# The first unit's score maxima from unstacked key halves in row tiles, with their loads moved among the last projections

## The chip, the cores and the metric

The kernel runs on one core of one Trainium2 chip. A core has five engines with instruction streams of their own: TensorE (PE, with its weight loads shown as PEld), VectorE (DVE), ScalarE (ACT), GpSimd (POOL) and SyncE (SP), which here issues nearly all DMAs. The metric is the device time of one launch in microseconds, the median of several runs.

## The reference

Two independent blocks, joined along the last axis of the output (2048 x 896, float32):

```python
# A: a long convolution by FFT, kernel K from 256 complex modes per channel
K = 2.0 * jnp.einsum("dn,dnl->dl", C, P).real
y = jnp.fft.irfft(jnp.fft.rfft(u_t, 2 * L) * jnp.fft.rfft(K, 2 * L)[None], 2 * L)[:, :, :L]
a = y.transpose(0, 2, 1) + u * D_skip
# B: full attention, 16 heads of 28, sequence 2048, float32
qkv = (x @ wqkv).reshape(B, S, 3, H, Dh).transpose(2, 0, 3, 1, 4)
scores = jnp.einsum("bhqd,bhkd->bhqk", q, k) * Dh ** -0.5
b = (softmax(scores) @ v, heads joined) @ wo
```

The change touches block B alone: the row maxima of the scores of one of its units, which the softmax subtracts.

## The kernel before, in words

The 16 heads form four groups g of four heads j, and the 2048 queries four chunks c of 512. A *unit* is one group and one chunk: u = 4 g + c, 16 units. For each unit the kernel first finds the maximum of every query's 2048 scores, writes its negative into spare rows of the query tile (so that the score matmul already subtracts it), and then walks through the keys in 16 steps: scores, exponential on ScalarE, product with the values.

The work up to the first exponential stands in one block with three strands.

*Projections* (`transposes`, `qk_proj`, `v_proj`). For each chunk c the input is transposed, split into a part `xh` that TensorE's fast float32 format holds exactly and a rest `xl`, and multiplied with weights that are split the same way (`wh`, `wl`). A `qk_proj` is 12 matmuls into one PSUM bank of 512 columns, followed by `evac`: ScalarE writes the high part, VectorE the low part of the result into `hl`, and SP stores `hl` to DRAM (`k_d` for keys, `q_d` for queries). There are two `hl` buffers and three PSUM banks for this (`w_tile`). The order in the last chunk is four value projections, then for each group its keys and its queries. For chunks 0 and 1 of the keys, `evac` also forms the difference of the two halves of the chunk (`kb`, `dhl`) and stores it to `kd_d`.

*Seeds* (`seeds`). Eight rounds prepare the modes of block A on VectorE, ScalarE and GpSimd (tiles `tri`, `sg`, `qhat`, `px`); each ends with two stores, `sd<-sg` and `sd<-qhat`.

*Maxima of unit 0* (`max_mm`). When the projections are through, SP and ScalarE load the keys of group 0 back as four tiles `khat` of 128 rows, in which high and low parts are stacked (`load_k`, four issues for each head; ScalarE issues those of the first two heads, SP the others), then the queries of unit 1 and the values. The queries of unit 0 and the differences of group 0 are loaded earlier (`load_q(0)`, `load_kd(0)`). One matmul over the 128 stacked rows gives a tile of 128 queries by 512 keys. Each of the 16 pairs of head j and query tile t has four such tiles: `kc` 0 is the product with the difference of two key halves, `kc` 1 with the second of these halves, `kc` 2 and 3 are plain keys. ScalarE reads `kc` 0 through a relu into `rl`; VectorE adds `rl` to `kc` 1 and takes the maximum in the same instruction (max(a, b) = b + relu(a - b)); `kc` 2 and 3 are read by VectorE with a plain maximum. Five PSUM banks are used in turn. `max_join`, `max_end` and `max_put` combine the results, turn them and store them into the query tile with two issues `qhat<-mh`.

Up to here a scheduler places the instructions: it moves them within the engines' streams by its own estimate, so program order is not the order on the engines. Behind this block the order is kept as written: three tiles of unit 1's maxima (12 matmuls), then the steps of unit 0, each with one tile of maxima of the unit that follows.

DMAs use eight completion semaphores in turn, so an issue waits until the one eight before it in that order has landed; SP takes its issues strictly in order.

## Time and profile before

| | |
|---|---|
| median of 3 runs | 1362.64 us (1361.73 to 1366.7) |
| the profiled execution's own time | 1363.72 us |
| its span, first to last instruction | 1361.9 us |
| granted TensorE clock, mean | 0.976 |
| PE, DVE, ACT, POOL busy | 91%, 73%, 71%, 62% |

The profile gives start times in us from the first instruction. A row of the chain of waits has start, length, engine, destination tile and the helper's line, which is the same for every instruction here (L75), so groups are known by their tiles: `pm` and `pt` are PSUM banks of projections and maxima, `hl` the evacuated projections, `khat` keys, `qhat` queries (and, in the seeds, a borrowed buffer), `kdif` the differences, `mx`, `rl`, `m`, `mh` the maxima, `pss` the scores, `p` the exponentials, `sg` and `tri` the seeds, `sd` their place in DRAM. In a timeline a row has start, length, engine, operation, destination and sources. SPq is SP's DMA issue; its length is the issue, not the transfer.

### The profile page before, as it was taken

The numbers are of one execution on the slowest core, as the hardware profiler recorded it, in microseconds if no ns is written. First come the engines' busy times: TensorE is split into PE (matmuls) and PEld (weight loads), VectorE is DVE, ScalarE is ACT, GpSimd is POOL, SyncE is SP. The second block draws the span as 40 slices with busy tenths as digits, with TensorE's granted clock in tenths as the row PEclk, the third lists the DMA queues.
The fourth block names the chain that finished last, engine by engine and source line by source line (L and its number), as shares of the span: only waits on it lengthen the run. The fifth ranks groups of instructions, "written<-read, shape, count | busy, mean of one in ns | idle before, by whom it ended". The sixth has DMA issues, their size and how long they took to land.

```text
span 1361.9 us, 33142 instructions
## 1 busy us (share of the span) xinstructions
PE 1243.9 (91%) x12625; PEld 709.8 (52%) x12625; DVE 991.3 (73%) x2138; ACT 966.1 (71%) x2067; POOL 839.5 (62%) x705
## 2 busy tenths in 40 slices
PE   6878885799999999999999999999998999998997
PEld 5657762455555555555555555555555545544433
DVE  5897886877777777777788888888887766857311
ACT  4876752488888888888888887878786655655553
POOL 3685681278877878878888988888895111202221
PEclk9988987899999999999999999999999999999999
DMA  6677669636675545378534233632325534636476
GB/s 197 199 261 266 225 212 271 179 74 150 147 164 118 128 135 159 111 202 198 162 94 97 56 73 86 146 79 67 79 65 140 189 116 161 206 111 203 138 192 176
DMA packets 200089, 205.36 MB, mean 151 GB/s; under 512 B 95993, under 2 KB 158521, under 8 KB 197881
## 3 DMA queue, kind: packets, MB, share of 16 engines
q1 hardware_dynamic: 199544, 201.13, 53.2%
q10 hardware_dynamic: 384, 2.10, 0.6%
q8 instruction: 100, 1.64, 0.5%
q14 instruction: 61, 0.49, 0.1%
HBM read 120.73 MB, written 82.18 MB: 149 GB/s over the span
## 4 chain that ended last, share of the span: by engine, by line
PE 61%; DVE 17%; ACT 12%; issue 3%; DMA 3%; POOL 3%; SPq 0%; ACTq 0%; DVEq 0%; POOLq 0%
PE pm L75 35%; PE po L75 13%; PE pss L75 12%; ACT p L75 6%; DVE mx L75 4%; DVE g L75 2%; DVE tri L75 2%; ACT rl L75 2%; DVE p L75 2%; POOL qhat L75 1%; DVE pr L75 1%; DVE zg L75 1%; DVE rl L75 1%; DVE sg L75 1%; ACT tri L75 1%
## 5 line engine op out<-in xcount | busy, mean ns | idle before, releaser
L75 ACT ACTIVATE p<-pss 128x512 f32<-128x512 f32 x1024 | 565.4, 609 | 138.5 <-PE pss L75 127.5
L75 PE MATMUL pss<-qhat,khat 128*128 128x512 f32 x1024 | 403.1, 400 | 3.3 <-ACT p L75 3.3
L75 DVE TENSOR_REDUCE mx<-pm 128x1 f32<-128x512 f32 x500 | 321.4, 683 | 116.3 <-PE pm L75 115.1
L75 PE MATMUL pm<-khat,qhat 128*128 128x512 f32 x749 | 330.1, 444 | 41.4 <-DVE mx L75 36.5
L75 POOL TENSOR_TENSOR e<-e,sdb 128x256 f32<-128x256 f32 x168 | 201.8, 1201 | 171.9 <-ACT e L75 162.9
L75 PE MATMUL po<-p,v 128*32 128x512 f32 x2048 | 271.9, 599 | 0.0
L75 POOL TENSOR_TENSOR e<-e,eu 128x256 f32<-128x256 f32 x168 | 248.1, 1477 | 13.2
L75 PEld LDWEIGHTS pm<-khat,qhat 128*128 128x128 f32 x749 | 142.0, 190 | 216.0 <-DVE mx L75 79.8
L75 PEld LDWEIGHTS pss<-qhat,khat 128*128 128x128 f32 x1024 | 191.1, 189 | 46.7 <-ACT p L75 11.2
L75 DVE CUSTOM_DVE_ANT_0 rl<-pm,rl 128x512 f32<-128x512 f32 x249 | 171.4, 688 | 48.3 <-ACT rl L75 43.8
L75 POOL TENSOR_TENSOR eu<-e,sdb 128x256 f32<-128x256 f32 x168 | 201.7, 1201 | 0.0
L75 DVE TENSOR_TENSOR g<-g,zg 128x128 f32<-128x128 f32 x392 | 162.9, 416 | 46.3 <-ACT zg L75 41.3
L75 ACT ACTIVATE rl<-pm 128x512 f32<-128x512 f32 x249 | 151.2, 607 | 20.7 <-PE pm L75 18.8
L75 POOL TENSOR_TENSOR p<-pr,pr 64x448 f32<-64x448 f32 x32 | 40.9, 1277 | 191.6 <-DVE pr L75 180.5
L75 PE MATMUL pm<-kdif,qhat 128*128 128x512 f32 x249 | 101.6, 408 | 2.2 <-DVE mx L75 1.5
L75 PEld LDWEIGHTS pm<-e,g 128*32 128x32 f32 x3584 | 63.0, 110 | 52.8 <-issue 30.8
L75 DVE TENSOR_TENSOR zg<-g,zg 128x128 f32<-128x128 f32 x224 | 87.5, 391 | 1.9
L75 PEld LDWEIGHTS po<-p,v 128*32 128x32 f32 x2048 | 56.6, 110 | 42.7 <-issue 38.0
L75 PE MATMUL pm<-xh,wh 112*128 112x512 f32 x128 | 56.8, 448 | 22.3 <-DVE hl L75 10.8
L75 PE MATMUL pm<-e,g 128*32 128x64 f32 x3584 | 72.5, 220 | 0.0
L75 ACT ACTIVATE y<-pm 128x448 f32<-128x448 f32 x48 | 26.3, 548 | 63.0 <-PE pm L75 30.7
L75 DVE TENSOR_TENSOR pr<-pm,ub 128x448 f32<-128x448 f32 x64 | 37.0, 619 | 32.7 <-PE pm L75 32.7
(137 smaller groups left out, 1571.8 us busy)
## 6 DMA issues: line engine op xcount, KB each, us to landing
sdb<-sd SPq DMA_DIRECT2D x56, 336.0 KB
qhat<-q SPq DMA_DIRECT2D x64, 256.0 KB
khat<-k SPq DMA_DIRECT2D x56, 256.0 KB
sd<-sg SPq DMA_DIRECT2D x8, 1456.0 KB
k<-hl SPq DMA_DIRECT2D x16, 512.0 KB
q<-hl SPq DMA_DIRECT2D x16, 512.0 KB
mw<-in_mw SPq DMA_DIRECT2D x16, 512.0 KB
sd<-qhat SPq DMA_DIRECT2D x8, 896.0 KB
```

Of the source, the lines that this page charges most:

```text
L75: i = f(*args, **kw)
```

## The change

Unit 0's maxima no longer use the stacked tiles. Five tiles `own_*` of 128 rows by 2 x 512 hold the high and the low parts of all four heads side by side: the queries of unit 0, the differences of the halves of the first two chunks (`d`), the second halves of these chunks (`b`), and the same two for the other chunks. SP loads them among the last projections, at the slots in `OWN`. They lie where the projections' `y_p` pool lay, which is closed at the first key projection of the last chunk.

Since the halves are not stacked, a score tile is the sum of four products (high and low of queries with high and low of keys), each over the 32 rows of one head (`own_max`): 256 matmuls instead of 64, issued for two heads in turn, whose rows lie in different 32-row strips of the array.

All keys are now read in pairs (`PAIRS` = 2): `kc` 0 and 2 are differences and go through ScalarE's relu, `kc` 1 and 3 are second halves and go through VectorE's add-and-maximum. For this the second difference is needed for group 0, so `evac` forms it for chunks 2 and 3 too (`kd2_d`); its temporaries `kb` and `dhl` now come from the `rl` ring.

The weights `wh`, `wl` are four tiles in the buffers that `khat` takes later, and all four `load_k(0, ...)` are issued by SP.

In the order that the scheduler gives the changed kernel, SP's stream near the end of the projections is: the store of the last chunk's first keys, `sd<-sg`, `own_q` and the first difference, the first query store, `sd<-qhat`, the first second-halves tile (two issues), the second group's key and query stores, a row block of `qhat`, the third group's key store, another row block, the second difference and the other second-halves tile (two issues), the third group's query store, `sd<-sg`, two row blocks, the fourth group's key store, `sd<-qhat`, its query store, 16 `khat`, 4 `qhat`, 4 `v`, the last `sd<-sg` and `sd<-qhat`, and then `qhat<-mh`. On TensorE six matmuls of the first own pair stand ahead of the last but one projection and the other two ahead of the last one. On ScalarE the two relu reads of this pair stand between the evacuations of the second group's queries and the third group's keys.

```diff
--- before.py
+++ after.py
@@ -42,6 +42,7 @@
 SGB, XB, XL = 2, 5, 4
 K0, KP, KD, UP = 0, 3.5, 5, 3
 A0, A1 = 26, 34
+OWN, KIND, PAIRS = (31, 31, 32, 34, 34), "dbdb", 2
 
 N1 = 32
 N2 = 64
@@ -103,6 +104,7 @@
     dram = ctx.enter_context(tc.tile_pool(name="dram", bufs=1, space=DRAM))
     k_d = [dram.tile([2, 128, L], F32, name=f"k_{g}") for g in range(G)]
     kd_d = [dram.tile([2, 128, CQ], F32, name=f"kd_{g}") for g in range(G)]
+    kd2_d = dram.tile([2, 128, CQ], F32, name="kd2")
     q_d = [[dram.tile([2, 128, CQ], F32, name=f"q_{g}_{c}") for c in range(NQ)] for g in range(G)]
     sd_d = [dram.tile([BO, 128, SDF], F32, name=f"sd_{o}") for o in range(NO)]
     yu_d = dram.tile([128, N1, D], F32, name="yu_d")
@@ -130,6 +132,7 @@
     q_p = pool(att, "q_p", side="right")
     v_p = pool(att, "v_p", side="right")
     kd_p = pool(att, "kd_p", side="right")
+    k0_p = pool(k0_st, "k0_p", side="right")
 
     def mm32(o, w, x_, start, stop, at=0):
 
@@ -140,10 +143,10 @@
 
     kt_g, kd_g, q_u, m_u, mh_u, o_u, rl_u = {}, {}, {}, {}, {}, {}, {}
 
-    def load_k(g, j, p, queue=nc.sync):
+    def load_k(g, j, p):
         t = p.tile([128, L], F32R, name="khat", bufs=HG)
         for r in range(4):
-            queue.dma_start(t[32 * r:32 * r + 32, :].bitcast(F32), k_d[g][r % 2, 32 * j:32 * j + 32, :])
+            nc.sync.dma_start(t[32 * r:32 * r + 32, :].bitcast(F32), k_d[g][r % 2, 32 * j:32 * j + 32, :])
         kt_g.setdefault(g, []).append(t)
 
     v_g = {}
@@ -169,24 +172,30 @@
 
     def max_mm(u, i, kc, ps=w_tile):
 
-        if i == 0 and kc == 0:
-            m_u[u] = q_p.tile([128, HG, 4, 3], F32, name="mx", bufs=2)
         j, t = divmod(i, 4)
         pm = ps()
         q, kt = q_u[u][:, j, t * 128:(t + 1) * 128], kt_g[u // NQ][j]
-        mx = m_u[u][:, j, t, max(kc - 1, 0):max(kc - 1, 0) + 1]
         if kc == 0:
             nc.tensor.matmul(pm, q, kd_g[u // NQ, j], start=True, stop=True)
-            rl_u[u, i] = kd_p.tile([128, CQ], F32, name="rl", bufs=2)
-            nc.scalar.activation(rl_u[u, i], pm, AF.Relu)
         elif kc == 1:
             kb = kt.rearrange("p (c s n) -> p c s n", c=NQ, s=2)[:, :2, 1, :]
             nc.tensor.matmul(pm.rearrange("p (c n) -> p c n", c=2), q, kb, start=True, stop=True)
-            rl = rl_u.pop((u, i))
-            nc.vector.tensor_tensor_reduce(rl, pm, rl, 1.0, -3.0e38, ALU.add, ALU.max, mx)
         else:
             nc.tensor.matmul(pm, q, kt[:, kc * CQ:(kc + 1) * CQ], start=True, stop=True)
-            nc.vector.tensor_reduce(mx, pm, axis=AX.X, op=ALU.max)
+        max_read(u, i, kc, pm)
+
+    def max_read(u, i, kc, pm, pairs=1):
+        if u not in m_u:
+            m_u[u] = q_p.tile([128, HG, 4, 4 - pairs], F32, name="mx", bufs=2)
+        j, t = divmod(i, 4)
+        if kc // 2 < pairs and kc % 2 == 0:
+            rl_u[u, i] = kd_p.tile([128, CQ], F32, name="rl", bufs=2)
+            nc.scalar.activation(rl_u[u, i], pm, AF.Relu)
+        elif kc // 2 < pairs:
+            rl = rl_u.pop((u, i))
+            nc.vector.tensor_tensor_reduce(rl, pm, rl, 1.0, -3.0e38, ALU.add, ALU.max, m_u[u][:, j, t, kc // 2:kc // 2 + 1])
+        else:
+            nc.vector.tensor_reduce(m_u[u][:, j, t, kc - pairs:kc - pairs + 1], pm, axis=AX.X, op=ALU.max)
 
     def max_join(u):
         m_u[u, 1] = q_p.tile([128, HG * 4], F32, name="m1", bufs=2)
@@ -212,7 +221,6 @@
         s_p = pool(sst, "s_p")
         x_p = pool(xst, "x_p")
         y_p = pool(wst, "y_p", side="right")
-        w_p = pool(wst, "w_p", side="right")
         ps_w[0] = pool(st, "ps_w", 1, PSUM)
         ps_t = pool(st, "ps_t", 2, PSUM)
         ps_n = pool(st, "ps_n", 2, PSUM)
@@ -227,12 +235,12 @@
                 nc.sync.dma_start(xns[c, h], xs[:, 2 * h:2 * h + 2, :])
 
         load_x(0)
-        wh = w_p.tile([CK, 2, NCK, H, 32], F32R, name="wh")
-        wl = w_p.tile([CK, 2, NCK, H, 32], F32R, name="wl")
+        wh, wl = ([k0_p.tile([128, L], F32R, name="khat", bufs=HG)[:CK].rearrange("p (k h e) -> p k h e", k=NCK, h=H)
+                   for _ in range(2)] for _ in range(2))
         vh = y_p.tile([CK, NCK, D], F32R, name="vh")
         vl = y_p.tile([CK, NCK, D], F32R, name="vl")
-        for w in (wh, wl):
-            nc.gpsimd.memset(w[:, :, :, :, DH:].bitcast(F32), 0.0)
+        for w in wh + wl:
+            nc.gpsimd.memset(w[:, :, :, DH:].bitcast(F32), 0.0)
         vst = [x_p.tile([128, H, 32], F32, name=f"vst{i}") for i in range(2)]
         for t in vst:
             nc.gpsimd.memset(t[:, :, DH:DH + 1], 1.0)
@@ -271,8 +279,8 @@
         for k in range(NCK):
             for s in (1, 0):
                 src = wns[k][:, s, :].rearrange("p (h e) -> p h e", e=DH)
-                nc.scalar.activation(wh[:, s, k, :, :DH], src, AF.Copy)
-                nc.vector.tensor_tensor(wl[:, s, k, :, :DH], src, wh[:, s, k, :, :DH].bitcast(F32), ALU.subtract)
+                nc.scalar.activation(wh[s][:, k, :, :DH], src, AF.Copy)
+                nc.vector.tensor_tensor(wl[s][:, k, :, :DH], src, wh[s][:, k, :, :DH].bitcast(F32), ALU.subtract)
             nc.scalar.activation(vh[:, k, :], wns[k][:, 2, :], AF.Copy)
             nc.gpsimd.tensor_tensor(vl[:, k, :], wns[k][:, 2, :], vh[:, k, :].bitcast(F32), ALU.subtract)
 
@@ -450,7 +458,7 @@
             n = 0
             for k in range(NCK):
                 for w_, x_ in ((wh, xh), (wl, xh), (wh, xl)):
-                    nc.tensor.matmul(pp, w_[:, s, k, hs, :].rearrange("p h e -> p (h e)"), x_[k],
+                    nc.tensor.matmul(pp, w_[s][:, k, hs, :].rearrange("p h e -> p (h e)"), x_[k],
                                      start=n == 0, stop=n == 3 * NCK - 1)
                     n += 1
 
@@ -463,16 +471,16 @@
                 else:
                     nc.scalar.activation(th, pp, AF.Copy)
                     nc.vector.tensor_tensor(tl, pp, th.bitcast(F32), ALU.subtract)
-                if s == 1 and c < 2:
+                if s == 1 and (c < 2 or g == 0):
                     HC = CQ // 2
-                    kb = y_p.tile([128, HC], F32, name="kb")
-                    dhl = y_p.tile([128, 2, HC], F32R, name="dhl")
+                    kb, dhl = (kd_p.tile([128, CQ], F32, name="rl", bufs=2) for _ in range(2))
+                    kb, dhl = kb[:, :HC], dhl.bitcast(F32R).rearrange("p (i l) -> p i l", i=2)
                     dh, dl = dhl[:, 0], dhl[:, 1]
                     nc.scalar.activation(kb, pp[:, HC:], AF.Copy)
                     nc.vector.tensor_tensor(kb, pp[:, :HC], kb, ALU.subtract)
                     nc.scalar.activation(dh, kb, AF.Copy)
                     nc.gpsimd.tensor_tensor(dl, kb, dh.bitcast(F32), ALU.subtract)
-                    nc.sync.dma_start(kd_d[g][:, :, c * HC:(c + 1) * HC].rearrange("i p l -> p i l"), dhl.bitcast(F32))
+                    nc.sync.dma_start((kd_d[g] if c < 2 else kd2_d)[:, :, c % 2 * HC:(c % 2 + 1) * HC].rearrange("i p l -> p i l"), dhl.bitcast(F32))
                 nc.sync.dma_start((k_d[g][:, :, c * CQ:(c + 1) * CQ] if s == 1 else q_d[g][c]).rearrange("i p l -> p i l"),
                                   hl.bitcast(F32))
             return evac
@@ -492,10 +500,43 @@
                 nc.sync.dma_start(v_d[c][:, :, t], vs.rearrange("p (g h) e -> p g (h e)", g=G))
             return evac
 
+        own, own_p = {}, []
+
+        def own_open():
+            wst.close()
+            own_p.append(pool(wst, "own_p", side="right"))
+
+        def own_load(n):
+
+            own[n] = t = own_p[0].tile([128, 2, CQ], F32R, name=f"own_{n}")
+            f = lambda d: d.rearrange("i p l -> p i l")
+            if n == "q":
+                nc.sync.dma_start(t.bitcast(F32), f(q_d[0][0]))
+            elif KIND[n] == "d":
+                nc.sync.dma_start(t.bitcast(F32), f(kd_d[0] if n == 0 else kd2_d))
+            elif KIND[n] == "b":
+                for c in range(2):
+                    c0 = (n - 1 + c) * CQ + CQ // 2
+                    nc.sync.dma_start(t[:, :, c * CQ // 2:(c + 1) * CQ // 2].bitcast(F32), f(k_d[0][:, :, c0:c0 + CQ // 2]))
+            else:
+                nc.sync.dma_start(t.bitcast(F32), f(k_d[0][:, :, n * CQ:(n + 1) * CQ]))
+
+        def own_max(t, js, kc, ps):
+            pms = [p() for p in ps]
+            for n, (a_, b_) in enumerate(((0, 0), (0, 1), (1, 0), (1, 1))):
+                for j, pm in zip(js, pms):
+                    r = slice(32 * j, 32 * j + 32)
+                    nc.tensor.matmul(pm, own["q"][r, a_, t * 128:(t + 1) * 128], own[kc][r, b_, :],
+                                     start=n == 0, stop=n == 3, tile_position=(32 * j, 0))
+            for j, pm in zip(js, pms):
+                max_read(0, 4 * j + t, kc, pm, PAIRS)
+
         work = []
         for c in range(NQ):
             jobs = [lambda c=c, s=s, g=g: qk_proj(c, s, g) for g in range(G) for s in (1, 0)]
             v_jobs = [lambda c=c, t=t: v_proj(c, t) for t in range(4)]
+            if c == NQ - 1:
+                jobs[0] = (lambda f: lambda: (own_open(), f())[1])(jobs[0])
             jobs = v_jobs + jobs if c == NQ - 1 else jobs + v_jobs
             jobs[0] = (lambda c, f: lambda: (transposes(c), f())[1])(c, jobs[0])
             if c + 1 < NQ:
@@ -516,6 +557,9 @@
         for i in range(2):
             ahead[A1 + i].append(lambda i=i: load_q(0, range(2 * i, 2 * i + 2)))
 
+        for t, n in zip(OWN, ("q", 0, 1, 2, 3)):
+            ahead[t].append(lambda n=n: own_load(n))
+
         def project():
 
             e = work.pop(0)() if work else None
@@ -531,18 +575,20 @@
                 f()
             if t + 1 == PW:
                 project()
-                wst.close()
-                k0_p = pool(k0_st, "k0_p", side="right")
                 for j in range(HG):
-                    load_k(0, j, k0_p, nc.scalar if j < 2 else nc.sync)
+                    load_k(0, j, k0_p)
                 load_q(1)
                 for c in range(NQ):
                     load_v(0, c)
         xst.close()
         more = [lambda: ps_t.tile([128, CQ], F32, name="pt")] * 2 + [w_tile] * 3
-        for i in range(16):
-            for kc in range(4):
-                max_mm(0, i, kc, more[(4 * i + kc) % 5])
+        n_ = 0
+        for t in range(4):
+            for js in ((0, 1), (2, 3)):
+                for kc in range(4):
+                    own_max(t, js, kc, [more[(n_ + i) % 5] for i in range(2)])
+                    n_ += 2
+        wst.close()
         max_join(0)
         max_end(0, ps_t.tile([128, CQ], F32, name="pt"))
         max_put(0)
```

## The prediction

> **What bounds the kernel now.** I read the page's span, then the chain of waits between the last projections and the first exponential, then a table by stage, then the DMA queue of SP and the window of the DMA engines. The whole run is 1361.9 us of span; the execution itself took 1363.72 us, 1.1 us above the median of 1362.64 that is shown. The change touches only the stage up to about 260 us; behind it the instruction order is unchanged, so what counts is when the first exponential starts.
>
> ```profile
> span 1361.9 us, 33142 instructions
> ```
>
> The chain of waits (start, length, what it was):
>
> ```profile
> 196.12 7.99 PE pm L75 x24
> 204.11 6.44 DMA khat<-k
> ...
> 210.93 6.78 DMA qhat<-q
> ...
> 225.82 0.60 DVE rl L75
> 226.42 1.21 DVE mx L75 x3
> ...
> 250.79 0.21 DVE m L75
> ...
> 258.59 0.60 ACT rl L75
> ```
>
> ```profile
> 260.50 1.09 ACT L75 ACTIVATE p<-pss 128x512 f32<-128x512 f32 x2
> ```
>
> The last two projections end at 204.1 us. Then TensorE stands until 217.9, because keys and queries of the first unit are still in the DMA. The 64 maxima of the unit follow up to 250.8, paced by VectorE: three reads per tile, 0.60 us each (1.81 us for one rl and two mx). The join, twelve matmuls of unit 1 and the table load fill 250.8 to 260.5, where the first exponential starts (the last row is from the timeline). Now the stages, in columns PE, PEld, DVE, ACT, POOL busy, then the granted clock, DMA share, GB/s:
>
> ```profile
> 193.00:196.00 3.00, 0.00 (x0) 0.00 (x0) 2.05 (x4) 3.00 (x6) 0.98 (x1) 0.74 0.16 61
> 196.10:204.10 8.00, 7.98 (x24) 6.25 (x24) 6.74 (x16) 3.01 (x10) 6.53 (x12) 0.68 0.84 266
> 204.10:217.90 13.80, 0.26 (x2) 0.08 (x1) 3.39 (x6) 2.23 (x6) 3.67 (x4) 0.65 1.04 286
> 217.90:250.80 32.90, 26.01 (x64) 12.76 (x64) 29.28 (x65) 9.55 (x16) 0.00 (x0) 0.89 0.97 270
> ```
>
> The reader should see two things. VectorE has no slack from 217.9 to 250.8 (29.28 of 32.90 us). And the DMA engines are full from 204 to nearly 250. The next fence says what stands in that queue (SP's issues, start and length) and when it runs dry (window 240 to 256 in 40 slices of 0.4 us: the 9s end in the twentieth slice, at about 248.2).
>
> ```profile
> 199.42 0.38 SPq L75 DMA_DIRECT2D k<-hl  x1
> ...
> 210.57 0.80 SPq L75 DMA_DIRECT2D qhat<-q  x2
> ...
> 215.45 11.04 SPq L75 DMA_DIRECT2D khat<-k  x8
> 226.97 3.82 SPq L75 DMA_DIRECT2D qhat<-q  x4
> 231.75 3.83 SPq L75 DMA_DIRECT2D v<-v  x4
> ...
> 237.74 0.37 SPq L75 DMA_DIRECT2D sd<-qhat  x1
> 251.67 1.26 SPq L75 DMA_DIRECT2D qhat<-mh  x2
> ```
>
> ```profile
> DMA  9999999999999999999941000000000010077799
> ```
>
> The maxima go back into the query rows by qhat<-mh, and no score of the unit can start before these land. Before, they are issued at 251.67 into an empty queue.
>
> **The change part by part.** *Reads.* Both key halves in pairs: per tile two reads on ScalarE (0.60 us, the rl row at 258.59) and two on VectorE (0.60) instead of one and three. 16 tiles make 19.3 us on each engine, where VectorE had 33 us (217.9 to 250.8). Alone this would be worth up to 13 us, and it is off the limit afterwards.
>
> *Matmuls.* 64 matmuls over 128 rows become 256 over 32 rows (four products of hi and lo), in pairs of heads on two row strips. No row strip runs in the trace of before, so I bound one of them by the nearest rows:
>
> ```profile
> 197.57 0.63 PE L75 MATMUL pm<-xh,wh 112*128 112x512 f32 x1
> 197.99 0.63 PE L75 MATMUL pm<-xh,wl 112*128 112x512 f32 x1
> ...
> 201.36 0.40 PE L75 MATMUL pm<-xh,wh 112*128 112x512 f32 x1
> 201.59 0.39 PE L75 MATMUL pm<-xh,wl 112*128 112x512 f32 x1
> ```
>
> ```profile
> 278.92 0.86 PE po L75 x8
> ```
>
> Start to start, a full-width matmul of 512 columns takes 0.23 us at full clock and 0.42 at half. Eight on four column strips take 0.86 us, 0.108 each, so strips do overlap. Lower end 0.117 (two strips fully overlapped), upper end 0.23 (no overlap). I take 0.125, as the strip row lies near the lower end: 31 us, and 3 us for the first 24, which the built order does not interleave by strips. The Trainium skill, "TensorE: Matmul & The Clock Gate", section Part 3 on row and column tiling, gives 3.07 times for four row tiles at 512 columns; by 77% efficiency it would be 0.15 us each, 39 us, an estimate that no run here shows yet.
>
> *Where they start.* The loads that the maxima need no longer follow the last projection: the queries, both differences and both key halves come as five tiles of 512 KB on SP (seven issues: the two key tiles take two each), queued between the seed stores, the hl stores and the rows of the first unit's queries. In the built order the last pieces (second difference, second half) stand right behind the store that was issued at 199.42 (k<-hl of the third head group). So the 13.8 us hole goes, if SP gets to that store as early as now.
>
> *It does not.* The built order puts two things ahead of it. First, VectorE now takes the low part of the query projection before it (second group) after three sg operations that stood behind it before:
>
> ```profile
> 195.38 0.69 DVE L75 TENSOR_TENSOR hl<-pm,hl 128x512 fp32r<-128x512 f32 x1 [0.57 <-ACT hl L75]
> ...
> 198.65 0.74 DVE L75 SCALAR_TENSOR_TENSOR hl<-pm,kones,hl 128x512 fp32r<-128x512 f32 x1
> ```
>
> It moves from 195.4 to after 198.65, plus 0.4 for the added difference (below): until about 199.7, where its bank comes free and the last but one projection can start (196.12 before). Second, ScalarE stands at two relu reads of the first pair before it may evacuate that third group, and TensorE finishes this pair only behind the last but one projection. So: 199.7 plus 12 matmuls at 0.42 (TensorE has been idle, clock 0.74 and 0.68 in the rows 193 to 204) is 204.8; two more pair matmuls, 205.6; two reads of 0.60, 206.9; evacuation by ScalarE and VectorE, 0.60 and 0.74, 208.3. The store that SP issued at 199.42 leaves at about 208.3, 8.9 us later, and everything behind it on SP with it. The last projection waits for the same bank and ends at 208.3 + 5.1 = 213.4 instead of 204.1. If TensorE is at full clock, 2.3 us of this goes (12 x 0.19); if the reads cost nothing, 1.2 us more.
>
> *The added differences* (two more groups):
>
> ```profile
> L75 ACT ACTIVATE kb<-pm x8: 363/374/387, 23.5 to 100.9; 128x256 f32<-128x256 f32 x8
> L75 DVE TENSOR_TENSOR kb<-pm,kb x8: 404/417/426, 24.4 to 102.3; 128x256 f32<-128x256 f32 x8
> L75 ACT ACTIVATE dhl<-kb x8: 401/416/425, 24.8 to 102.8; 128x256 fp32r<-128x256 f32 x8
> L75 POOL TENSOR_TENSOR dhl<-kb,dhl x8: 740/1168/1932, 25.3 to 106.9; 128x256 fp32r<-128x256 f32 x8
> ```
>
> Twice 0.79 us on ScalarE, 0.42 on VectorE, 1.2 on POOL and a store of 256 KB. The one near 180 us lies where VectorE sets the chain, so 0.4 us (in the sum above); the earlier one hides in the DMA waits of 193 to 196. At most 2 x 2.4 us if none is hidden.
>
> *DMA.* What drains when: rates come from two windows, 32-partition loads (226 to 232) and stores and 128-partition loads (240 to 242):
>
> ```profile
> DMA packets 244, 1.34 MB, mean 223 GB/s; under 512 B 81, under 2 KB 81, under 8 KB 81
> ```
>
> ```profile
> DMA packets 430, 0.78 MB, mean 391 GB/s; under 512 B 46, under 2 KB 96, under 8 KB 429
> ```
>
> The sizes in KB per issue (q<-hl is as k<-hl, and a v load of 128 rows by 512 floats is 256 KB):
>
> ```profile
> qhat<-q SPq DMA_DIRECT2D x64, 256.0 KB
> khat<-k SPq DMA_DIRECT2D x56, 256.0 KB
> sd<-sg SPq DMA_DIRECT2D x8, 1456.0 KB
> k<-hl SPq DMA_DIRECT2D x16, 512.0 KB
> ...
> sd<-qhat SPq DMA_DIRECT2D x8, 896.0 KB
> ```
>
> From the store at 199.42 to the first qhat<-mh stand: 16 khat and 7 qhat issues (1.18 us each), four hl stores (1.34), four v loads (0.67), two seed stores sd<-sg (3.8) and two sd<-qhat (2.35). That is 27.1 + 5.4 + 2.7 + 7.6 + 4.7 = 47.5 us, from 199.4 to 246.9; the queue ran dry at 248.2, so the sum holds within 1.3 us. The change adds two of its five loads behind that store (2.7 us); the other three go into the hole from 193 on (share 0.16). From 208.3: 208.3 + 47.5 + 2.7 + 1.0 = 259.5 us, when the last seed store has gone. The built order has qhat<-mh behind it on the same queue. All khat loads are on SP now, ahead of it too, while eight were issued by ScalarE.
>
> *The sum.* TensorE ends its maxima at 213.4 + 31 + 3 - 1 (the eight done before) = 246.4, and qhat<-mh is ready to issue about 1 us later (250.8 to 251.67 before). It lands only behind the queue: 259.5 + 1.5 = 261.0 (0 to 3 us for the landing; I take the middle), and then one score and the exponential, 0.8 us: 261.8 instead of 260.5. The twelve matmuls of unit 1 and the table load, which stood in the path before, lie in the shadow of this wait; if it goes, they are late next, and the start is the end of the maxima plus 9.7 us (250.8 to 260.5), 256.1. So the gain of 14 us at the start and 13 us of reads is given back, first to later projections, then to a full DMA queue. 1363.72 + 1.3 = 1365.0 in the profiled execution's terms, 1364 in terms of the median.
>
> **The rivals.** *A, slower: the row strips do not overlap.* The start is set by TensorE once the maxima end after 252.1, that is from 0.155 us per matmul, not far above the value taken. At 0.23, 248 matmuls end at 213.4 + 57.0 = 270.4, the first exponential starts at 280.1, 1383 us. For it: no row strip in the trace, and the same 57 us if the strips overlap but the clock stays at half. Against it: the overlap of the column strips, and TensorE would have no idle time to lose its clock in. At 0.18 it is 1370.
>
> *B, faster: the projections do not slip.* If the relu reads find their pair done early and TensorE is warm, the store leaves at about 201, the queue is dry at 252 and the exponential starts at 254.5: 1356.6. For it: the six early pair matmuls may fill the idle time of 193 to 196 and keep the clock up; against it: the order of the built ScalarE queue.
>
> *C, the early maxima do not start early,* since the second difference and half land late (about 215 us by the queue above). It costs TensorE about 2 us at 213 to 217 and changes nothing as long as the DMA ends later.
>
> The Trainium skill, "TensorEngine Tiling (Array Packing)", section Key Properties, says that a change of tiling mode drains TensorE; that is a few changes here, and no row prices it.
>
> **How the numbers follow.** The forecast has 0.48, A 0.26, B 0.22, C within the forecast and the rest 0.04. A measurement of this kernel can tell about 0.5%, 6.8 us, from no change. Of B, 0.17 is over 6.8 us faster, with 0.01 of the forecast; of A 0.24 is over 6.8 us slower (the rest stays at 0.16 to 0.18 us a matmul), with 0.06 of the forecast if both unknown costs of the added groups show. That makes 0.18 faster, 0.52 same, 0.30 slower. The range goes from B's 1356 to 1377, a matmul of 0.21 us in A; about 0.1 is left out on each side. The forecast alone: 1359 to 1369.
>
> **What would show it.** Right: the last projection ends near 213; a DMA row of 9s until about 259; the first p waiting for DMA qhat<-mh; own matmuls at 0.12 to 0.13 us start to start. Wrong: k<-hl of the third group at about 201 (B); or TensorE busy with own tiles until 260 or later, at 0.2 us each or a granted clock near 0.5 (A). Were qhat<-mh to land before the last seed store is through, the queue would not be in order, and the start would be 256.

## The result and the profile after

The changed kernel takes 1379.93 us (median of four runs, 1379.77 to 1380.37), the kernel before 1363.58 beside it: a ratio of 1.0129, interval 1.0102 to 1.0155. It is slower, and outside the predicted range of 1356 to 1377. The profiled execution took 1379.77 us with a span of 1378.0. The first exponential starts at 273.18 instead of 260.50, so 12.7 of the 16.1 us are lost where the prediction looked for them; the other 3.4 come later (see the end of the experiments).

```profile
273.18 1.09 ACT L76 ACTIVATE p<-pss 128x512 f32<-128x512 f32 x2
```

The chain of waits of the changed kernel, from the last projections to the first exponential (start, length, engine, tile):

```profile
194.27 5.49 PE pm L76 x12
199.76 0.77 PE pt L76 x2
...
201.01 0.59 ACT rl L76
201.60 0.58 ACT hl L76
202.21 0.76 DVE hl L76
203.01 6.28 PE pm L76 x16
...
210.48 0.66 DVE hl L76
211.18 2.08 PE pm L76 x4
...
260.05 1.30 PE pm L76 x7
...
265.85 5.40 PE pm L76 x9
271.28 0.60 ACT rl L76
```

From 211.18 to the end of the maxima at 261.4 the chain is TensorE but for 1.5 us, where it was VectorE before. No DMA stands in it. The table by stage says why (PE, PEld, DVE, ACT, POOL busy with counts, which take in what overlaps an edge, then granted clock, DMA share, GB/s):

```profile
201.00:207.60 6.60, 4.58 (x11) 3.62 (x12) 5.22 (x13) 2.05 (x7) 2.81 (x3) 0.50 0.58 153
207.60:211.00 3.40, 1.68 (x7) 0.78 (x5) 2.75 (x7) 1.13 (x4) 3.24 (x4) 1.00 0.99 331
211.00:220.00 9.00, 7.34 (x29) 5.46 (x31) 2.68 (x8) 2.29 (x5) 0.07 (x1) 0.50 1.06 355
220.00:230.00 10.00, 10.00 (x51) 8.13 (x50) 3.99 (x14) 3.12 (x7) 0.00 (x0) 0.50 1.06 280
...
240.00:250.00 10.00, 10.00 (x60) 7.50 (x56) 4.38 (x13) 3.37 (x6) 0.00 (x0) 0.50 1.03 247
250.00:261.40 11.40, 11.40 (x59) 8.20 (x55) 4.79 (x16) 4.56 (x8) 0.00 (x0) 0.50 0.55 195
```

TensorE is busy without a pause from 220 to 261.4, and its granted clock is 0.50 all that time. It had been 1.00 for a moment (207.6 to 211.0), in which TensorE then stood for 1.91 us, waiting for the evacuation that frees a PSUM bank (timeline); it never came back.

```profile
211.18 1.22 PE L76 MATMUL pm<-own,own_q 32*128 32x512 f32 x2 [1.91 <-DVE hl L76]
```

The last 244 of the 256 own matmuls need 50 us, about 0.20 each. VectorE and ScalarE, 4.4 and 3.4 of 10 us, are far from the limit. SP's issues and the DMA window from 240 to 260 (40 slices of 0.5 us), both of the changed kernel, show that the queue isn't the limit either:

```profile
202.99 0.38 SPq L76 DMA_DIRECT2D k<-hl  x1
...
245.90 0.37 SPq L76 DMA_DIRECT2D sd<-qhat  x1
263.88 1.27 SPq L76 DMA_DIRECT2D qhat<-mh  x2
```

```profile
DMA  8979999999999999999999999999999610000000
```

The queue runs dry at about 255.5; the maxima are stored only at 263.88, into an empty queue.

### The profile page after: what moved, and what is told of

It is laid out like the page before. It is cut to its first block, busy times and chain, and to the rows that moved or that the text cites. A ratio compares the mean times of both kernels' runs of the same rounds, so it can differ in the third digit from the quotient of the medians.

```text
span 1378.0 us, 33610 instructions
## 1 busy us (share of the span) xinstructions
PE 1273.5 (92%) x12817; PEld 736.6 (53%) x12817; DVE 984.9 (71%) x2140; ACT 976.6 (71%) x2087; POOL 838.7 (61%) x709
## 4 chain that ended last, share of the span: by engine, by line
PE 64%; DVE 15%; ACT 12%; issue 3%; POOL 3%; DMA 2%; SPq 0%; ACTq 0%; DVEq 0%; POOLq 0%
PE pm L76 38%; PE po L76 13%; PE pss L76 12%; ACT p L76 6%; DVE mx L76 3%; DVE g L76 2%; ACT rl L76 2%; DVE p L76 2%; PE pt L76 2%; DVE tri L76 1%; DVE pr L76 1%; POOL qhat L76 1%; DVE qhat L76 1%; DVE sg L76 1%; DVE zg L76 1%
## 5 line engine op out<-in xcount | busy, mean ns | idle before, releaser
L76 DVE TENSOR_REDUCE mx<-pm 128x1 f32<-128x512 f32 x480 | 308.4, 683 | 108.3 <-PE pm L76 107.1
L76 PE MATMUL pm<-khat,qhat 128*128 128x512 f32 x720 | 318.5, 444 | 39.6 <-DVE mx L76 35.2
L76 PEld LDWEIGHTS pm<-khat,qhat 128*128 128x128 f32 x720 | 136.5, 190 | 211.3 <-DVE mx L76 76.1
L76 DVE CUSTOM_DVE_ANT_0 rl<-pm,rl 128x512 f32<-128x512 f32 x260 | 178.6, 689 | 64.7 <-ACT rl L76 43.5
L76 ACT ACTIVATE rl<-pm 128x512 f32<-128x512 f32 (+1 forms) x268 | 159.9, 598 | 33.1 <-PE pm L76 23.0
L76 PE MATMUL pm<-xh,khat 112*128 112x512 f32 x256 | 93.9, 451 | 23.5 <-DVE hl L76 11.4
L76 PE MATMUL pm<-kdif,qhat 128*128 128x512 f32 x240 | 96.8, 403 | 0.7 <-DVE pr L76 0.2
L76 PEld LDWEIGHTS pm<-xh,khat 112*128 112x128 f32 x256 | 54.6, 219 | 39.9 <-DVE hl L76 13.5
```

The costliest lines, as they stand in the source:

```text
L76: i = f(*args, **kw)
```

## The experiments

The question was why 256 matmuls on two row strips keep half the clock, and whether that is the whole error. The theories, as the expectations number them: 1, the clock follows the number of rows at work, and two strips of 32 are too few; 2, matmuls of 32 rows never release it; 3, strips do not overlap beyond two; 4, the stage starts cold, and a clock that is full stays full while there is no gap; 5, formed after the first eight runs, what counts is the share of rows at work over some microseconds. All runs in one table (clock and first exponential from the run's profile, the time a median, or one value for e2, e3, e4, f4 and g3; the kernel before has its first exponential at 260.5, and 1361.8 to 1363.6 us beside these runs):

| run | what it changes | clock in the own stage | first exponential | time, us |
|---|---|---|---|---|
| after | | 0.50 | 273.2 | 1379.9 |
| e1_four | four strips in turn, eight banks | 0.50 and 1.00 in turn | 270.5 | 1373.2 |
| e2_full | the same count over 128 rows | 1.00 | 277.7 | 1380.2 |
| e3_rows64 | the same count over 64 rows | 0.50 | 329.9 | 1436.3 |
| e4_warm | 48 full-row matmuls added | 1.00 | 262.8 | 1366.6 |
| f3_warm16 | 16 of them, ahead of all | 1.00, 0.50 from 219 | 273.0 | 1380.2 |
| f1_order | written order, first key pairs first | 0.50 from 208 | 265.7 | 1370.2 |
| f2_late | f1 with two seed stores later | 0.50 from 211 | 267.2 | 1374.0 |
| f4_pairs1 | f1 with one pair instead of two | 0.50 from 210 | 267.6 | 1375.5 |
| g0_banks | f1 with other banks | 0.50 from 210 | 259.3 | 1364.6 |
| g1_one | g0 with one full-row matmul a group | 1.00 from 213 | 275.2 | 1377.7 |
| g2_two | g0 with two a group | 1.00 from 214 | 283.4 | 1385.1 |
| g3_cold | after with two a group | 1.00 from 219 | 282.2 | 1382.6 |
| h0_hi | after with one product of four | 0.50 | 257.0 | 1360.9 |
| h1_fill | g0 with full rows in its two gaps, then eight banks | 1.00 to 239 | 257.1 | 1363.9 |
| h2_hi | g0 with one product of four | 0.50 | 256.1 | 1357.7 |
| h3_hi_late | h2 with two seed stores later | 0.50 | 254.8 | 1359.5 |

**How many rows.** e1_four takes four heads at a time, over eight PSUM banks instead of five:

```diff
-            for js in ((0, 1), (2, 3)):
-                for kc in range(4):
-                    own_max(t, js, kc, [more[(n_ + i) % 5] for i in range(2)])
+            for kc in range(4):
+                own_max(t, (0, 1, 2, 3), kc, [more[(n_ + i) % 8] for i in range(4)])
```

> Edit: the maxima of unit 0 are issued for all four heads in turn (four row strips of 32, eight PSUM banks in rotation) instead of two heads and five banks. Theory 1 (the clock follows how many rows of the array work at a time, and two strips are too few): the granted clock goes to about 1.0 a few us into the own matmuls, which then take 0.06 us each or wait for the reads (22 us for all); they end near 235 us, and the start of the exponentials is set by the DMA queue, about 256 us, so 1359 to 1362 us, 18 to 21 us below the changed kernel. Theory 2 (32-row matmuls never release the clock, however many strips): clock 0.5 throughout, 0.107 us each, end near 243 us; the time is much the same, since the DMA queue still ends later. Theory 3 (the strips beyond two do not overlap): 0.214 us each as in the changed kernel, end near 262 us, 1380 us.

e2_full and e3_rows64 keep count and order, and let each matmul run over all 128 rows or over the first 64. What they subtract in unit 0 is another value, so they are read for time alone.

```diff
-  matmul(pm, own["q"][r, a_, ...], own[kc][r, b_, :], ..., tile_position=(32 * j, 0))
+  matmul(pm, own["q"][:, a_, ...], own[kc][:, b_, :], ...)                            # e2
+  matmul(pm, own["q"][:64, a_, ...], own[kc][:64, b_, :], ..., tile_position=(0, 0))  # e3
```

> Edit: each of the 256 matmuls contracts over all 128 rows (the four heads summed), so the value that is subtracted in unit 0 is another one; count, banks and order are kept. Theory 1 and theory 2: the granted clock is about 1.0 in this stage, matmuls do not overlap and take 0.23 us each, 60 us in all, first exponential near 281 us, about 1387 us. Theory 4 (the clock stays at half because the stage starts cold, whatever runs in it): clock 0.5, 0.43 us each, 110 us, about 1437 us.

> Edit: each of the 256 matmuls contracts over rows 0 to 63 (two heads summed; the subtracted value is another one), one after the other, so that 64 rows work at any time, as with two overlapping strips. Theory 1: clock 0.5 as in the changed kernel, now 0.43 us each, 110 us, first exponential near 330 us, about 1437 us. If the number of working rows does not matter but their tiling in strips of 32 does: clock 1.0, 0.23 us each, about 1387 us.

The same stage in these three (columns as above), e1 first, then e2 and e3:

```profile
232.00:238.00 6.00, 5.16 (x42) 4.08 (x35) 2.62 (x8) 2.78 (x6) 0.00 (x0) 0.50 1.06 219
238.00:244.00 6.00, 4.59 (x41) 2.88 (x36) 3.83 (x11) 2.79 (x6) 0.00 (x0) 0.93 1.04 219
```

```profile
232.00:238.00 6.00, 6.00 (x28) 4.97 (x27) 1.89 (x5) 2.05 (x4) 0.00 (x0) 1.00 1.00 225
```

```profile
232.00:238.00 6.00, 6.00 (x15) 4.58 (x14) 1.31 (x4) 1.09 (x2) 0.00 (x0) 0.50 1.04 227
```

With TensorE equally full (6.00 of 6), 128 rows hold the full clock and 64 rows one at a time stay at half. The two did not enter the stage alike: the projections had raised e2's clock to 1.00 at 204.9, while e3's fell to 0.50 at 213.0. So this compares holding with not raising; but projections over 112 rows, equally full, do raise the clock (in after, 3.41 us without a pause at 0.50, then 1.00 from 207.6). Occupancy alone doesn't decide, then, and it isn't the 32-row form as such. e3 also settles the overlap: without it a matmul takes 0.42 us at half clock; two strips took half of that. Four strips start four matmuls every 0.43 us at half clock, 0.11 each (e1_four, from 229.8), so theory 3 falls; and they raise the clock at times, though they wait for reads in between (5.16 and 4.59 of 6 us), so theory 2 falls too. e1 ends 11 us above what theory 1 let expect, at 1.0073 (1.005 to 1.0096) of before.

**History.** e4_warm puts 48 full-row matmuls (three runs of 16, results unused) at the start, of which the built order places 32 ahead and 16 among the first own ones; f3_warm16 puts only 16, all ahead.

```diff
+        for i in range(3):                       # f3_warm16: range(1)
+            pd = w_tile()
+            for n in range(16):
+                nc.tensor.matmul(pd, own["q"][:, 0, :128], own[0][:, 0, :], start=n == 0, stop=n == 15)
```

> Edit: 48 matmuls over 128 rows are added, 32 ahead of the own maxima and 16 among the first of them, results unused. Theory 1: the clock rises to 1.0 during these and falls back to 0.5 within some 5 us of two-strip work; own matmuls end about 10 us later than in the changed kernel, about 1388 us. Theory 4: once at 1.0 it stays there, own matmuls take 0.107 us each, 27 us in all, end near 252 us, about 1370 us.

> Edit: 16 matmuls over 128 rows ahead of the own maxima, results unused; everything else as in the changed kernel. Theory 4 (two strips keep a full clock but can't raise a half one): the clock reaches 1.0 before or within these and stays there, 0.107 us per own matmul; the maxima end near 244 us, the DMA queue near 253 us sets the rest, first exponential 254 to 256 us, 1358 to 1361 us, at or just below the kernel before. If the 16 that stood amid the own matmuls in the run with 48 were what kept the clock: back to 0.5 after some 7 us, end of the maxima near 260 us, about 1378 us.

e4_warm by stage:

```profile
232.00:238.00 6.00, 6.00 (x56) 4.86 (x54) 4.03 (x14) 3.96 (x8) 0.00 (x0) 1.00 1.04 228
244.00:250.00 6.00, 6.00 (x53) 4.71 (x52) 4.32 (x13) 3.61 (x7) 0.00 (x0) 1.00 1.05 280
```

The same two strips, back to back, now keep 1.00 for over 25 us, at 0.117 each (205 start from 226 to 250): 48 more matmuls, and 13 us less than after. f3_warm16 starts its own matmuls warm too (stages, then one row of its timeline):

```profile
213.00:218.00 5.00, 5.00 (x32) 3.71 (x33) 2.48 (x6) 1.69 (x3) 0.00 (x0) 1.00 1.08 363
...
219.50:225.00 5.50, 5.49 (x24) 4.86 (x27) 1.31 (x4) 2.13 (x4) 0.00 (x0) 0.50 1.11 376
```

```profile
219.51 1.21 PE L76 MATMUL pm<-own,own_q 32*128 32x512 f32 x2 [0.79 <-DVE mx L76]
```

The clock is gone at 219.1, until 270, and nothing is gained (1.0125, 1.0096 to 1.0155). TensorE stands there for 0.79 us, as VectorE was late with one read, but this stand is not shown to be the cause. e4_warm kept its clock through one nearly as long:

```profile
225.00 0.73 PE L76 MATMUL pm<-own,own_q 32*128 32x512 f32 x3 [0.69 <-ACT rl L76]
```

In f3_warm16, before the stand, the strips had come one at a time, from 215.8 to 217.5 with starts 0.23 to 0.34 us apart. So theory 4 holds in its first half, and "no gap" is not the condition; the last section takes this up.

**The written order.** f1_order keeps the order of the maxima as written on all engines, and takes the first key pairs of all tiles before the second, whose loads land later. f2_late also moves the last two seed stores behind `qhat<-mh`. f4_pairs1 is f1 without the second difference, so that `kc` 2 and 3 are plain keys read by VectorE.

```diff
+        nc.kept = KEPT["a"]
+        for half in range(2):
             for t in range(4):
                 for js in ((0, 1), (2, 3)):
-                    for kc in range(4):
+                    for kc in (2 * half, 2 * half + 1):
```

```diff
+                if t >= n_stage - 2:             # f2_late
+                    seeds_late.append(f)         # called behind max_put(0)
-OWN, KIND, PAIRS = (31, 31, 32, 34, 34), "dbdb", 2
+OWN, KIND, PAIRS = (31, 31, 32, 34, 34), "dbkk", 1   # f4_pairs1
```

> Edit: the own maxima keep their written order on all engines, so none of them stands between the projections, and the pair of the first key halves is taken for all tiles before the second. Theory 4: TensorE goes from the projections into the own maxima without a gap and at full clock, 27 us, end near 232 to 236 us; the store of the third group's keys leaves near 199 to 201 us, the DMA queue runs dry near 250 to 252 us and qhat<-mh lands behind it; first exponential 252 to 255 us, 1355 to 1358 us. If the clock is lost at a gap between the last projection and the own maxima, it stays at 0.5 and the maxima end near 262 us, about 1378 us.

> Edit: as the run with the written order, and the last two seed stores (2.4 MB) are issued behind qhat<-mh instead of ahead of it. If the wait of qhat<-mh in SP's queue is what gives the gain back, it lands some 6 us earlier, near 246 us, and the first exponential starts at 248 to 252 us (the loads of unit 1's queries and its twelve matmuls then decide), 2 to 5 us below the run with the written order. If that queue isn't the limit: no difference.

> Edit: as the run with the written order, but only the first two key chunks are read in pairs (VectorE reads three of four score tiles, as before the change), and the second difference is neither formed nor loaded. VectorE's 48 reads take 29 us, TensorE's matmuls 27 us; the maxima end 2 to 4 us later than with both pairs, near 236 to 240 us, still ahead of the DMA queue: within 2 us of the run with the written order. If the reads are the limit: 5 us or more above it.

f1_order's timeline of TensorE:

```profile
205.77 1.19 PE L76 MATMUL pt<-own,own_q 32*128 32x512 f32 x8
...
209.91 2.07 PE L76 MATMUL pm<-own,own_q 32*128 32x512 f32 x7 [2.73 <-DVE hl L76]
```

The projections end at 205.8 at full clock and the own matmuls start without a pause, and then one PSUM bank is still held by an evacuation (2.73 us). From 208 on the stage runs at 0.50; the first exponential is still 7.5 us ahead of after's. The start gives little of this (16 matmuls are done at 213.6, in after 12 at 214.0); the last 240 take 41.0 us instead of 47.7 at the same clock, as the strips overlap more closely in this order. f2_late stands 4.70 us at the same place and gains nothing: with the store of the maxima ahead of 6 us of seed stores, the first exponential is not earlier (267.2 against 265.7), so the queue wasn't the limit, and in the profiled executions some 4.5 us more than in f1 are lost later. f4_pairs1, a single run, reaches the first exponential 1.9 us later than f1 and takes 5.4 us more in all; VectorE is nearly full there (13.86 of 15 us):

```profile
240.00:255.00 15.00, 15.00 (x93) 11.70 (x88) 13.86 (x23) 0.00 (x0) 0.00 (x0) 0.50 1.00 296
```

So reading the second half in pairs is worth about 2 us of this stage while TensorE sets the pace; the rest of the 5.4 us is lost behind it, and its cause was not looked for.

**Banks and fillers.** g0_banks takes two banks `pn` into the turn and only every fifth from the projections' ring. g1_one and g2_two add one or two full-row matmuls ahead of every group of eight own ones (eight ahead of groups 1 and 5); g3_cold adds two to every group of the changed kernel and nothing else.

```diff
-        more = [pt] * 2 + [w_tile] * 3
+        more = [pt] * 2 + [pn] * 2 + [w_tile]
+            for n in range(fill):       # g1 1, g2 and g3 2; not in g0
+                nc.tensor.matmul(pd, own["q"][:, 0, :128], own[0][:, 0, :], start=True, stop=True)
```

> The kernel with the written order of the maxima (f1_order), with the two banks pn as well and only one bank of the projections' in every five, so that the second and third group of eight own matmuls need not wait for the last evacuations (2.73 us before the row at 209.91 in that run). Theory 4 (a clock that is full stays full as long as the row strips run without a gap): if the new banks close the gap, the clock stays at 1.0 from 200.5 on, 32 groups of 8 x 0.107 = 27.5 us end the maxima near 237, the first exponential starts between 253 (where the DMA queue is the limit) and 256, 1356 to 1359. What I expect rather: the reads of the first tiles on ScalarE stand behind an evacuation that waits for its buffer until 210.94, so a gap of 1.5 to 3 us only moves to the third or fourth group, the clock is lost between 208 and 214 as before, and the time is 1368 to 1372.

> As g0_banks, with one matmul over all 128 rows (its result is not used) ahead of every group of eight own matmuls, and eight instead of one ahead of the first and of the fifth group, where the reads are late. Theory 5 (what counts in a window of 3.4 us is the share of rows at work: 1 for a matmul over 128 rows, a half for two strips, none in a gap; the full clock is kept and regained well above one half and not at one half): a group has 0.21 + 0.86 us with a mean share of 0.6, the gaps are filled with full rows, so the clock stays at 1.0 or comes back within two windows; 32 x 1.07 + 14 x 0.22 = 37.3 us from 205.8, maxima end at 243 to 247, first exponential at 253 to 257, 1356 to 1361: faster than both kernels. Against it (any two-strip stretch of 0.86 us at half clock 1.7 us holds the clock down, however it is mixed): half clock, 2.14 us a group, maxima end near 280, 1390 or more.

> As g1_one with two full-row matmuls ahead of every group. Theory 5: mean share of rows 0.67, clock 1.0 with more room for gaps; 32 x 1.28 + 12 x 0.22 = 43.7 us, maxima end at 250 to 252, first exponential at 259.5 to 262, 1363 to 1366. If one full-row matmul per group is too few and two are enough, this one is faster than g1_one, which then has half-clock stretches; if neither is, 2.57 us a group, 1400 or more.

> The changed kernel in its own order and with its own banks, with two full-row matmuls ahead of every group and nothing else, so the stage starts at half clock as there (0.50 from 211.0 on). Theory 5: the share of rows is 0.67 instead of 0.50 at the same full occupancy, so the clock rises to 1.0 within two or three windows of 3.4 us and stays there unless a gap of more than 1.5 us comes; maxima end near 211.2 + 6 + 27 groups x 1.28 = 252, first exponential 260 to 264, 1366 to 1372, although 64 matmuls are added. If only an unmixed stretch of full-row matmuls lifts the clock (theories 1 and 2 in their strict form): half clock to the end, 32 x 2.57 = 82 us, first exponential near 303, 1410.

g3_cold by stage:

```profile
212.00:216.00 4.00, 3.56 (x8) 2.31 (x8) 0.44 (x1) 0.99 (x3) 0.00 (x0) 0.50 1.06 393
216.00:220.00 4.00, 4.00 (x14) 2.42 (x14) 1.30 (x3) 0.00 (x0) 0.00 (x0) 0.58 1.05 320
220.00:225.00 5.00, 5.00 (x26) 2.84 (x23) 0.00 (x0) 0.15 (x1) 0.00 (x0) 1.00 1.09 341
```

The clock rises from cold to 1.00 at 219.3, and it stays there to 274. The rise itself doesn't test the mixture, since the scheduler had put three groups' full rows in one stretch just ahead of it:

```profile
216.45 2.93 PE L76 MATMUL px<-own,own_q 128*128 128x512 f32 x6
```

What the run shows is that two full-row matmuls to eight own ones keep the clock, not that they raise it; that only an unmixed stretch raises it, as the strict form of theories 1 and 2 has it, is not refuted by this run. The times are 10 to 20 us above the expected ranges in all three: at the full clock a group takes 1.56 (g1_one) to 1.66 us (g2_two), where after's eight matmuls at half clock take 1.6. g2_two's timeline shows where it goes:

```profile
230.98 0.73 PE L76 MATMUL px<-own,own_q 128*128 128x512 f32 x2
231.64 0.49 PE L76 MATMUL pn<-own,own_q 32*128 32x512 f32 x1
...
232.76 0.73 PE L76 MATMUL px<-own,own_q 128*128 128x512 f32 x2
```

From one pair of full-row matmuls to the next is 1.78 us here and 1.66 on average (29 pairs from 220 to 268). Two at 0.227 (e2_full, 176 from 220 to 260) and eight at 0.117 (e4_warm) make 1.39; the other 0.27 to 0.39 us goes at the two changes between 128 rows and strips, 0.13 to 0.2 each. In g1_one the same sum gives 0.2. The prediction had named the Trainium skill, "TensorEngine Tiling (Array Packing)", section Key Properties, for the drain at a change of mode, as something that no row priced: these 0.13 to 0.2 us, 64 times over, fit it, though what TensorE does in them is not shown. g0_banks halves the stands of f1 (its timeline):

```profile
207.25 0.50 PE L76 MATMUL pt<-own,own_q 32*128 32x512 f32 x1 [0.94 <-ACT rl L76]
...
214.65 0.79 PE L76 MATMUL pm<-own,own_q 32*128 32x512 f32 x1 [1.07 <-DVE hl L76]
```

It loses the clock at 210 all the same, and still reaches 1.0012 (0.9997 to 1.0026): no difference from before.

**The sum without its wrong term.** h0_hi leaves out three of four products, in the changed kernel's own order; h2_hi does so in g0_banks, h3_hi_late also moves the two seed stores. The three left out hold a low part, so the value subtracted is rounded, which cancels in the softmax. h1_fill keeps all products, puts full rows only into g0's two gaps, and takes eight banks in turn from there on.

```diff
-            for n, (a_, b_) in enumerate(((0, 0), (0, 1), (1, 0), (1, 1))):
+            for n, (a_, b_) in enumerate(((0, 0),)):              # h0, h2, h3
-  own_max(t, js, kc, [more[(n_ + i) % 5] ...])
+  own_max(t, js, kc, [...], {4: 5, 14: 8}.get(n_, 0))             # h1: full rows ahead of these
```

> The changed kernel with one product instead of four for each own tile (high part times high part; the three products with a low part are left out, so the maxima that are subtracted are rounded, which a softmax with its own sum cancels). This takes away three quarters of the term that the prediction mis-sized and touches nothing else. If this term alone is the error, the rest of the sum must hold: 64 matmuls on two strips take at most 0.43 us a pair, 14 us even at half clock; reads of 19.3 us on each engine from about 211 end the maxima near 232 to 235; then the DMA queue is the limit, as in the forecast: it ran dry at 252.7 in the changed kernel, the maxima land at 254 and the first exponential starts at 254.5 to 256, 4.5 to 6 us before that of the kernel before: 1356 to 1360, near rival B. If something else in the change costs the time (the loads, the added differences, later steps), the time stays above 1365.

> The written order with the new banks (g0_banks) and full-row matmuls only where TensorE stood there: five (1.1 us) ahead of the third group of eight, before 207.25 in that run, and eight (1.7 us) ahead of the eighth, before 214.65; eight banks in turn afterwards. No full-row matmul stands among the others, so the strips change to full rows and back only twice. Theory 5 and e4_warm: without gaps the clock stays at 1.0 from 203 on; 32 x 0.86 + 2.8 + about 1 for the changes = 31.5 us from 204.2 to 206, maxima end at 236 to 239; the DMA queue (dry at about 252) is then the limit, first exponential at 253.5 to 256, 1355 to 1359. If a shorter stand still costs the clock (a bank or a read late by a few tenths): half clock from there on, 1.71 us a group, 1363 to 1372.

> g0_banks (written order, new banks) with the one product of h0_hi. The store of the third group's keys leaves at about 199.7 as in g0_banks, 3.3 us ahead of the changed kernel, so the DMA queue runs dry near 250 instead of 252.7; the maxima are through before 235. First exponential at 251 to 254, 1353 to 1358, 2 to 3 us below h0_hi. If the queue is not the limit even then, but the twelve matmuls of unit 1 and the table load behind the maxima (9.7 us after their end), the exponential starts near 245, 1346.

> h2_hi with the last two seed stores (6.2 us of DMA time by the sum of the prediction) behind the maxima's store on the queue. If the DMA queue is the limit of h2_hi, the maxima land 5 to 6 us earlier, first exponential at 246 to 249, 1348 to 1353. If it isn't, no change; and if the first steps of unit 0 need these stores (the loads that read them are issued right behind the maxima's store), up to 6 us are given back there.

(The 252.7 in these expectations, as the time at which after's queue ran dry, is misread: its DMA row above ends at 255.5.) The chain of waits of h0_hi:

```profile
237.18 9.66 DMA qhat<-q
...
246.93 0.78 PE pm L76
...
249.34 6.78 DMA qhat<-mh
...
256.20 0.77 PE pss L76
```

Now the forecast's picture is there: the own maxima are through at 237.4, TensorE stands for 9.5 us, and the chain is the DMA queue but for one tile of unit 1, up to `qhat<-mh`, which lands at 256.1. (The profile ties the second issue to VectorE's read at 249. But the maxima were ready at 238.0 and issued at 245.63, and they land 0.4 us behind the last seed store, so I take the queue for the cause.) The first exponential starts at 257.0, the time is 1360.9 us, 0.9976 (0.9961 to 0.9992) of before. h1_fill gets there with all four products (its stages):

```profile
221.80:236.00 14.20, 14.20 (x161) 11.92 (x155) 13.07 (x41) 11.80 (x20) 0.00 (x0) 1.00 1.03 222
236.00:239.00 3.00, 1.17 (x8) 0.47 (x6) 2.40 (x10) 1.36 (x3) 0.00 (x0) 0.99 1.03 223
```

Its matmuls take 0.092 us each at full clock (155 start in these 14.2 us), the maxima end at about 237 where g0's ended near 249, and the first exponential moves by 2.1 us only, since the queue is now the limit (`qhat<-mh` lands at 256.2 in its chain). Full rows and banks changed together, so what each gave is open. Its time, 1.0004 (0.9985 to 1.0023), cannot be told from g0's or from before. h2_hi has the lowest median, 1357.73 us, 0.9967 (0.9949 to 0.9984) of before: a gain of 0.3% over that kernel, and more over the changed one. h3_hi_late starts the exponentials 1.3 us earlier and cannot be told from h2_hi (1359.45 us; 0.9959, 0.9943 to 0.9975): once the maxima land earlier, the three tiles of unit 1 are late, whose queries stand in the same queue and land at 245.6.

Over all sixteen runs and the changed kernel, the profiled execution's time differs from before's as the first exponential does, within 3.4 us, but for f4_pairs1 with 4.7 and f2_late with 5.6. What makes these few us later on was not tried; after's 3.4 us belong to them.

## Why the prediction was wrong

*The step that failed* is the term "Matmuls": "I take 0.125 ... 31 us, and 3 us for the first 24". The strips do overlap, and at full clock they are faster than taken (0.117 in e4_warm, 0.092 in h1_fill). At 0.50 they take 0.20, 50 us. This is rival A by its second mechanism ("the same 57 us if the strips overlap but the clock stays at half"), with a chance of 0.26 and 1383 us; measured 1379.9. Its first mechanism, no overlap, is wrong. The argument against A, "TensorE would have no idle time to lose its clock in", failed twice. There was idle time, 1.91 us at 209.3, just when the clock had come; and a busy TensorE doesn't get the clock back on two strips. h0_hi shows that this term is the error: with a quarter of the matmuls and the rest of the program the same (the scheduler places it a little differently), the time falls by 19 us, below the forecast. e4_warm shows that the clock is what makes the term large: all 256 matmuls and 48 more, but at 1.00, take 13 us less than after.

The Trainium skill, "TensorE: Matmul & The Clock Gate", section Part 1 on the clock gate, gives the full clock after one window of about 3.4 us of sustained work. Behind projections over 112 rows the traces agree (after, 1.00 from 207.6); after's 41 us without a pause at 0.50 do not, nor does e3_rows64.

*The slip of the projections* was right in kind, too large in size. ScalarE did stand, 7.02 us, at the two relu reads ahead of the third group's evacuation:

```profile
200.52 1.08 ACT L76 ACTIVATE rl<-pt 128x512 f32<-128x512 f32 x2 [7.02 <-PE pt L76]
```

The store left at 203.0 instead of 208.3, 3.6 us later than before and not 8.9. The low part of the second group's queries, taken as 199.7 from the built order, was done at 194.2: the order was read rightly, the times of what stands before it were not. All later times of the forecast are 5.3 us too late for this.

*The DMA sum* held within 1.3 us: 47.5 + 2.7 + 1.0 = 51.2 us behind that store is 254.2, and the queue ran dry at 255.5. *That the queue is the limit* was wrong in the changed kernel and right in h0_hi: its store left at 201.4, plus 51.2, 1.5 and 0.8 is 254.9, and it measured 257.0. There the DMA sum is the term that was too short. The last seed store landed at 255.7 (an issue of SP waits for it) and not at 252.6, with loads issued from 249.9 on already in the queue; the maxima landed 0.4 us behind it, where 1.5 was taken.

```profile
255.69 0.31 SPq L76 DMA_DIRECT2D ua<-in_A_u  x1
```

*The twelve matmuls of unit 1* do not lie free in the shadow of that wait, as the prediction had it: their queries are in the same queue and land at 246.8 in h0_hi, so they end nearly as late as the maxima land.

*The reads* came out as worked out, and off the limit (VectorE 4.4 of 10 us). *The added differences* and rival *C* don't show in the chain. Rival *B*, faster because the projections do not slip, was half true (store at 203.0) and worth nothing, as TensorE was the limit.

## What to carry to other kernels

Price a matmul that fills only part of the rows at half the clock unless a row of such matmuls at full clock stands in a trace; that TensorE is busy says nothing here, the granted clock of the stage does. Two short strips kept a full clock here only where they started on it and ran closely overlapped with few waits, so banks and reads have to be ready before the first one; full-row fillers cost more than they brought when mixed in, and may pay in a gap (h1_fill, with more banks). And where a term is large, ask first whether it is needed: a maximum that a softmax subtracts need not be exact, and without its low parts the stage was off TensorE's limit at half clock.

## What the runs showed of the hardware

Two strips of 32 rows, fully back to back, do not raise the granted clock from 0.50 (41 us without a pause in after), nor does one tile of 64 (94 us in e3_rows64). Two strips keep it at 1.00 once it is there (26 us without a pause in e4_warm), and four strips raise it at times (e1_four). The length of a stand doesn't tell when the clock drops: f3_warm16 lost it beside 0.79 us, and h1_fill kept it through this one, behind eight full-row matmuls:

```profile
219.31 1.19 PE L76 MATMUL pt<-own,own_q 32*128 32x512 f32 x7 [1.51 <-DVE mx L76]
```

What does tell can be worked out from the traces, though no run was made to test it. The granted clock changes only on a grid of 3.41 us (in after at 194.0, 207.6, 211.0 and 272.5, which are 4, 1 and 18 steps apart). For each stretch of this grid, add up the matmuls, each with its rows divided by 128, times 0.427 us at half clock (the time from start to start in e3_rows64) or half of that at full clock, and divide by 3.41. This is the share of rows at work, an estimate from the starts in the traces. These are all stretches from 182 to 287 us in the changed kernel and the sixteen runs in which at least half of the matmuls are own ones or the full rows added to them:

| clock in the stretch | in the next one | stretches | share of rows |
|---|---|---|---|
| 1.00 | 0.50 | 23 | 0.34 and less |
| 1.00 | 1.00 | 91 | 0.37 and more |
| 0.50 | 0.50 | 138 | 0.72 and less |
| 0.50 | 1.00 | 5 | 0.78 and more |

Two fully overlapped strips make 0.50, between the two levels: enough to keep the clock and not enough to raise it. After's stage has 0.47 to 0.66 from 221 to 258. The stretch behind which f3_warm16 lost the clock has 0.25, g0_banks' 0.30; the stretches with the stands that e4_warm and h1_fill survived have 0.46 and 0.48. So theory 5 had the right quantity with one level where the traces show two. Stretches in which other matmuls prevail, some of them on column strips, do not separate as cleanly.

A change between 128 rows and 32-row strips goes with a loss of 0.13 to 0.2 us at full clock (g1_one, g2_two).
